# First chunk of a layer norm ahead of attention and MLP: the order of normalisation, statistics and piece copies on VectorE and ScalarE, and epsilon as the root's bias

## The chip, the cores and the metric

The kernel runs on one core of a Trainium2 chip. The metric is the device time of one execution in microseconds (us); several runs are made and the median is taken. The core has five engines with queues of their own: TensorE (PE, with its weight loads as PEld), VectorE (DVE), ScalarE (ACT), GpSimd (POOL) and SyncE (SP), which here issues the DMAs. They meet through semaphores only.

## The reference, cut to what matters

```
x: 2048 x 640
xn  = (x - mean(x)) / sqrt(var(x) + 1e-5)            # over the 640 columns
A   = sliding-window attention(xn @ wqkv) @ wo       # 32 heads of 20, window 256
B   = (gelu(xn @ w_gate) * (xn @ w_up)) @ w_down     # 640 -> 1728 -> 640
out = x + A + B
```

All of it is float32. The kernel splits a float32 operand into a high piece (a rounded copy, made by ScalarE) and a low piece (the remainder, by a subtraction on VectorE or GpSimd) and multiplies high by high, low by high and high by low.

## The kernel before

The 2048 rows are 16 tiles of 128 rows, and four tiles are a chunk. First every chunk is normalised, transposed and projected; attention, gate and up projections and the down projection follow. The change lies in the first of these stages, above all in its first chunk.

For a tile `xi` of 128 x 640, `ln_stats` (L119 to L121) makes mean and variance on VectorE: two statistics instructions and one that joins them into `mv`. `ln_sqrt` adds epsilon on VectorE (L126, `ve`) and takes the root on ScalarE (L127, `sq`). `ln_rstd` makes the reciprocal and one Newton step with four small VectorE instructions (L132 to L135): the reciprocal reads `sq`; the other three each read both `ve` and `rs` from SBUF. `ln_apply` (L139) subtracts the mean and multiplies, in place, over 640 columns.

```
        nc.vector.tensor_scalar(ve, mv[:, :, 1], EPS, None, op0=OP.add)
        nc.scalar.activation(sq, ve, AF.Sqrt)
```

`turn` (L156) then transposes 128-column blocks of the normalised tiles on TensorE into PSUM (`ps_t`), where the high piece `xh` is copied out by ScalarE (`high`, L292, in the first chunk, L164 in the others) and the low piece `xl` is subtracted by VectorE (`low`, L289 and L165). Weights are split by `split`: the high piece `wqh` on ScalarE (L74), the low piece `wql` on GpSimd (L75). `load_v` does the same with the value weights: `wvh` on ScalarE (L238), `wvl` on GpSimd (L239), five pieces of 320 columns each. GpSimd also fills constants: `mask`, `nm`, the ones columns of `v` (L249, L250), and `ones` (L365).

`first_chunk` is the only code that works on half a chunk at a time: tiles 0 and 1 (`ta`, the first pair) and tiles 2 and 3 (`tb`, the second pair). It projects two weight tiles, `w0` and `w5`, into the PSUM tiles `dn` (L296). Its TensorE order is: ten transposes of the first pair, five matmuls `w0` high by `xh`, five `w5` high by `xh`, five `w0` low by `xh`, six transposes of the second pair, five `w5` low by `xh`, four transposes, then forty more matmuls. Then come the value projections of the first tiles (`ps_v`, L82). The results go through `save_qk`, which splits them in pieces too (L215 on ScalarE, L216 on VectorE, L203 on ScalarE, L204 on GpSimd) and stores them. 64 small matmuls on a zero tile (L355, `ps_u`) run ahead of everything while the first tiles are loaded.

What sets the order: inside `first_chunk` the order on TensorE, ScalarE and VectorE is the order of the code, except where an independent instruction of another part (the `identb` copy L361, the `wvh` copies) is set between. GpSimd and SyncE there, and all engines in the chunks 1 to 3 behind it, are ordered by a scheduler from its own estimates. Each engine then works through its queue strictly in that order. From about 50 us on, the order of all engines is the same in both kernels.

Of the kernel before, what the change touches and what calls it, by code (L numbers as in the profile page):

```python
# [9 lines left out]
F32 = mybir.dt.float32  # L10
F32R = mybir.dt.float32r
BF = mybir.dt.bfloat16
AF = mybir.ActivationFunctionType
OP = mybir.AluOpType
# [7 lines left out]
KT = D // 128  # L22
# [3 lines left out]
EPS = 1e-5  # L26
# [19 lines left out]
def block_kernel(ctx, tc, x, xt, wqk, wv, wo, wgu, wd, wdl, out):  # L46
    nc = tc.nc

    const = ctx.enter_context(tc.tile_pool(name="const", bufs=1))
# [4 lines left out]
    nc.scalar.activation(one, one, AF.Sqrt)  # L54
    ident = const.tile([128, 128], F32, name="ident")
    make_identity(nc, ident)
    edge = ctx.enter_context(tc.tile_pool(name="edge", bufs=1, side="right"))
    edge.tile([128, 120], F32, name="edge")
    px = ExitStack()
# [11 lines left out]
    def split(pool, raw, shape, name, lo_eng, bufs=None):  # L71
        hi = pool.tile(shape, F32R, name=name + "h", tag=name + "h", bufs=bufs)
        lo = pool.tile(shape, F32R, name=name + "l", tag=name + "l", bufs=bufs)
        nc.scalar.activation(hi, raw, AF.Copy)  # L74
        lo_eng.tensor_tensor(out=lo, in0=raw, in1=hi.bitcast(F32), op=OP.subtract)  # L75
        return hi, lo
# [20 lines left out]
    vp = pr.enter_context(tc.tile_pool(name="vp", bufs=5, side="right"))  # L97
    st1 = pr.enter_context(tc.tile_pool(name="st1", bufs=1, side="right"))
    identb = st1.tile([128, 256], BF, name="identb")[:, 0:128]
    mask = st1.tile([128, 384], F32, name="mask")  # L100
    nc.gpsimd.memset(mask, 0.0)
    nc.gpsimd.affine_select(out=mask, in_=mask, pattern=[[1, 384]], compare_op=OP.is_ge,
# [9 lines left out]
    def ln_load(t, lp):  # L112
        xi = lp.tile([128, D], F32, name="xi", tag="xi", bufs=8)
        nc.sync.dma_start(xi, x[t * 128:(t + 1) * 128, :])
        return xi

    def ln_stats(xi, mv, lp):
        st = lp.tile([128, 2, 6], F32, name="st", tag="st", bufs=4)
        nc.vector.bn_stats(st[:, 0, :], xi[:, 0:320])  # L119
        nc.vector.bn_stats(st[:, 1, :], xi[:, 320:640])  # L120
        nc.vector.bn_aggr(mv, st)  # L121

    def ln_sqrt(mv, n, lp):
        ve = lp.tile([128, n], F32, name="ve", tag="ve", bufs=2)
        sq = lp.tile([128, n], F32, name="sq", tag="sq", bufs=2)
        nc.vector.tensor_scalar(ve, mv[:, :, 1], EPS, None, op0=OP.add)  # L126
        nc.scalar.activation(sq, ve, AF.Sqrt)  # L127
        return ve, sq

    def ln_rstd(ve, sq, n, lp):  # L130
        rs = lp.tile([128, n], F32, name="rs", tag="rs", bufs=4)
        nc.vector.reciprocal(rs, sq)  # L132
        nc.vector.tensor_tensor(out=ve, in0=ve, in1=rs, op=OP.mult)
        nc.vector.scalar_tensor_tensor(ve, ve, -0.5, rs, op0=OP.mult, op1=OP.mult)
        nc.vector.scalar_tensor_tensor(rs, ve, 1.5, rs, op0=OP.add, op1=OP.mult)  # L135
        return rs

    def ln_apply(xi, mv, rs):
        nc.vector.tensor_scalar(xi, xi, mv[:, 0:1], rs, op0=OP.subtract, op1=OP.mult)  # L139
# [11 lines left out]
    def turn(k, xs, where):  # L151
        n = len(xs)
        pool, tag = {"x": (psx, "ex"), "m": (psm, "mx"), "o": (pso, "o")}[where]
        ps = pool.tile([128, n * 128], F32, name="ps_t", tag=tag)
        for i in range(n):
            nc.tensor.transpose(ps[:, i * 128:(i + 1) * 128], xs[i][:, k * 128:(k + 1) * 128], ident)  # L156
        return ps
# [22 lines left out]
    def load_qk(t):  # L180
        raw = wrp.tile([128, KT, 128], F32, name="wr", tag="wr")
        nc.sync.dma_start(raw, wqk[t])
        return raw

    def split_qk(raw):
        return split(wp, raw, [128, KT, 128], "wq", nc.gpsimd)
# [98 lines left out]
    def first_chunk(xs, wr0, wr5, lp):  # L285
        halves = slice(0, 256), slice(256, 512)

        def low(k, ps, cs):
            nc.vector.tensor_tensor(out=xl[:, k, cs], in0=ps, in1=xh[:, k, cs].bitcast(F32), op=OP.subtract)  # L289

        def high(k, ps, cs):
            nc.scalar.activation(xh[:, k, cs], ps, AF.Copy)  # L292

        def part(ps, w, r, cs, first=False, last=False):
            for k in range(KT):
                nc.tensor.matmul(ps[:, cs], w[:, k, :], r[:, k, cs], start=first and k == 0,  # L296
                                 stop=last and k == KT - 1, skip_group_check=True)

        with tc.manual_schedule(engines=MANUAL):
            mv = [lp.tile([128, 2, 2], F32, name="mv", tag="mv", bufs=2) for _ in range(2)]  # L300
            ln_stats(xs[0], mv[0][:, 0, :], lp)
            ln_stats(xs[1], mv[0][:, 1, :], lp)
            va = ln_sqrt(mv[0], 2, lp)
            ln_stats(xs[2], mv[1][:, 0, :], lp)
            rs = ln_rstd(*va, 2, lp)
            ln_apply(xs[0], mv[0][:, 0, :], rs[:, 0:1])
            ln_apply(xs[1], mv[0][:, 1, :], rs[:, 1:2])
            ln_stats(xs[3], mv[1][:, 1, :], lp)
            w0 = split_qk(wr0)
            w5 = split_qk(wr5)  # L310
            ta = [turn(k, xs[0:2], "xmxmm"[k]) for k in range(KT)]
            dn = [psd.tile([128, C], F32, name="ps_d", tag="dn") for _ in range(2)]
            for k in range(KT):
                high(k, ta[k], halves[0])
                if k == 1:
                    vb = ln_sqrt(mv[1], 2, lp)
            for k in range(2):
                low(k, ta[k], halves[0])
            rs = ln_rstd(*vb, 2, lp)
            ln_apply(xs[2], mv[1][:, 0, :], rs[:, 0:1])  # L320
            ln_apply(xs[3], mv[1][:, 1, :], rs[:, 1:2])
            part(dn[0], w0[0], xh, halves[0], True)
            part(dn[1], w5[0], xh, halves[0], True)
            part(dn[0], w0[1], xh, halves[0])
            tb = [turn(0, xs[2:4], "o")]
            for k in range(2, KT):
                low(k, ta[k], halves[0])
            for k in range(1, 3):
                tb.append(turn(k, xs[2:4], "oxmxm"[k]))
            part(dn[1], w5[1], xh, halves[0])  # L330
            for k in range(3, KT):
                tb.append(turn(k, xs[2:4], "oxmxm"[k]))
            for k in range(KT):
                high(k, tb[k], halves[1])
            for k in range(KT):
                low(k, tb[k], halves[1])
            mv = lp.tile([128, 4, 2], F32, name="mv4", tag="mv4", bufs=2)
            for i, w in enumerate((w0, w5)):
                part(dn[i], w[0], xl, halves[0])
                part(dn[i], w[0], xh, halves[1])  # L340
                part(dn[i], w[1], xh, halves[1])
                part(dn[i], w[0], xl, halves[1], last=True)
                for j in range(2):
                    ln_stats(xs[4 + 2 * i + j], mv[:, 2 * i + j, :], lp)
                save_qk(5 * i, 0, dn[i])
        return w0, w5, mv

    v0 = []
    with tc.tile_pool(name="lp", bufs=1, side="right") as lp:
        xs = [ln_load(t, lp) for t in range(4)]  # L350
        warm = lp.tile([128, 256], BF, name="warm")[:, 0:128]
        nc.vector.memset(warm, 0.0)
        ps = psd.tile([128, C], F32, name="ps_u", tag="dn")
        for i in range(WARM):
            nc.tensor.matmul(ps[:, 0:128], warm, warm, start=True, stop=True)  # L355
        wr0, wr5 = load_qk(0), load_qk(5)
        prep = load_v(0, v0, lp)
        next(prep)
        xs += [ln_load(t, lp) for t in range(4, 8)]
        w0, w5, mv1 = first_chunk(xs, wr0, wr5, lp)  # L360
        nc.vector.tensor_copy(identb, ident)  # L361
        run(prep)
        v0 = v0[0]
        ones = lp.tile([2, 2 * C], BF, name="ones")
        nc.gpsimd.memset(ones, 1.0)  # L365
        for i in range(NK):
            for j in (0, 2):
                nc.sync.dma_start(ks[i][120:122, j:j + 2].rearrange("p j t -> p (j t)"), ones)
        for c in range(1, NC):
            ln_scale(xs[4 * c:4 * c + 4], lp, mv1 if c == 1 else None)  # L370
            ln_turn(4 * c, xs[4 * c:4 * c + 4])
            if c + 1 < NC:
                xs += [ln_load(t, lp) for t in range(4 * c + 4, 4 * c + 8)]
            if c == 2:
                raws1 = [load_qk(1), load_qk(6)]
            if c < NC - 1:
                run(*[proj_v(v0, 4 * c - 4 + i, None if i % 2 else (pso, "o")) for i in range(4)])
                run(proj_qk(0, w0, c), proj_qk(5, w5, c))
# [761 lines left out]
```

## Time and profile before

| | |
|---|---|
| median of 3 runs | 1117.17 us (1116.29 to 1118.18) |
| the profiled execution | 1116.69 us, its span 1115.0 us |
| TensorE busy | 1098.7 us, 99% of the span |
| VectorE, ScalarE, GpSimd busy | 637.7, 470.9 and 359.9 us |
| mean granted TensorE clock | 0.995 |

The page's chain is the work that ended last, followed back from the last instruction. A row of the timeline has the start, the length, the engine, the line and operation, what is written and read with its shape, a count where several were merged, and in brackets the idle time of the engine before it and what ended that. The start of an instruction is the moment at which the engine takes it up; one that cannot go on is shown as a long one. A row of the windows has, for each stretch of time, the length and the busy times of the five engines with their instruction counts, then the granted TensorE clock as a share of full speed, the DMA share and the GB/s.

### The profile page before, as it was taken

The page shows a single profiled execution, that of the slowest core. Times are in us where ns is not written, and L with a number is a line of the kernel's source. Part 1 is how long each engine was busy: PE and PEld are TensorE (multiplying, and loading weights), DVE is VectorE, ACT ScalarE, POOL GpSimd, SP SyncE. Part 2 cuts the span into 40 slices and gives each one's busy share as a digit, 9 for nine tenths or more (in the row PEclk, how much of TensorE's full clock was granted, in tenths as well). Part 3 has the DMA queues.
Part 4 walks back from the last instruction along what each step waited for, and adds up shares of the span by engine and source line. Part 5 has one row for each costly group of instructions (what it writes and reads, how often), then busy time and mean ns, then how long its engine had stood idle before and what let it go on. Part 6 is the DMA issues. An engine that isn't in the chain of part 4 may idle for free.

```text
span 1115.0 us, 19319 instructions
## 1 busy us (share of the span) xinstructions
PE 1098.7 (99%) x6802; PEld 837.6 (75%) x6802; DVE 637.7 (57%) x1736; ACT 470.9 (42%) x952; POOL 359.9 (32%) x504
## 2 busy tenths in 40 slices
PE   7999999999999999999999999999999999999998
PEld 7887666767668876667667676788888878788886
DVE  7856676757648577586777775566664350211203
ACT  4434554555555455645545454643323421211111
POOL 4122542644552233534323343311113313222230
PEclk8999999999999999999999999999999999999999
DMA  4642343543443314343242431342214835152431
GB/s 157 220 143 60 103 144 115 139 146 95 139 144 109 87 58 143 111 146 107 80 140 83 125 104 38 107 150 92 89 66 157 264 125 175 48 179 75 152 95 66
DMA packets 76145, 133.10 MB, mean 119 GB/s; under 512 B 12800, under 2 KB 33664, under 8 KB 76048
## 3 DMA queue, kind: packets, MB, share of 16 engines
q1 hardware_dynamic: 76048, 131.87, 37.6%
q8 instruction: 53, 0.87, 0.3%
q14 instruction: 44, 0.36, 0.1%
HBM read 86.31 MB, written 44.83 MB: 118 GB/s over the span
## 4 chain that ended last, share of the span: by engine, by line
PE 91%; DVE 4%; ACT 1%; DMA 1%; issue 1%; POOL 1%; SPq 0%; DVEq 0%; ACTq 0%; POOLq 0%
PE ps_d L82 28%; PE ps_w L942 23%; PE ps_g L851 11%; PE ps_o L484 7%; PE ps_e L462 7%; PE ps_m L410 6%; PE ps_v L82 6%; DVE junk L412 2%; PE ps_g L82 1%; PE ps_t L156 1%; PE ps_d L296 1%; ACT P L464 1%; PE ps_b L912 0%; DMA xi<-x 0%; DMA qs<-qd 0%
## 5 line engine op out<-in xcount | busy, mean ns | idle before, releaser
L412 DVE CUSTOM_DVE_ANT_0 junk<-ps_m,mask 128x384 bf16<-128x384 f32 (+2 forms) x512 | 271.2, 530 | 158.0 <-PE ps_m L410 120.0
L464 ACT ACTIVATE P<-ps_e 128x512 f32<-128x512 f32 (+2 forms) x384 | 197.5, 568 | 71.0 <-PE ps_e L462 64.6
L470 POOL TENSOR_SCALAR_AFFINE_SELECT P<-P 128x512 f32<-128x512 f32 x128 | 83.8, 655 | 221.1 <-ACT P L464 212.8
L82 PE MATMUL ps_d<-xh,wqh 128*128 128x512 f32 x510 | 150.4, 407 | 0.0
L82 PE MATMUL ps_d<-xh,wql 128*128 128x512 f32 x510 | 150.3, 407 | 0.0
L82 PE MATMUL ps_d<-xl,wqh 128*128 128x512 f32 x510 | 149.3, 406 | 0.0
L410 PE MATMUL ps_m<-ks,qs 120*128 120x128 bf16 (+1 forms) x704 | 120.9, 275 | 4.1 <-DVE mx L412 2.8
L921 POOL TENSOR_TENSOR ht<-hr,ht 128x512 fp32r<-128x512 f32 x52 | 69.2, 1337 | 172.1 <-ACT ht L919 142.9
L462 PE MATMUL ps_e<-qs,ks 122*128 122x128 bf16 (+2 forms) x704 | 112.5, 277 | 0.8 <-ACT P L464 0.6
L82 PEld LDWEIGHTS ps_d<-xl,wqh 128*128 128x128 f32 x510 | 92.9, 188 | 19.2 <-issue 2.4
L82 PEld LDWEIGHTS ps_d<-xh,wql 128*128 128x128 f32 x510 | 93.1, 189 | 18.0 <-issue 0.9
L82 PEld LDWEIGHTS ps_d<-xh,wqh 128*128 128x128 f32 x510 | 92.6, 188 | 17.2 <-ACT xh L164 0.3
L919 ACT ACTIVATE ht<-hr 128x512 fp32r<-128x512 f32 x56 | 35.1, 629 | 132.7 <-PE ps_w L942 80.8
L462 PEld LDWEIGHTS <-ks 122*128 122x128 bf16 x704 | 49.9, 98 | 54.6 <-issue 44.3
L473 POOL TENSOR_SCALAR_AFFINE_SELECT P<-P 128x512 f32<-128x512 f32 x112 | 74.2, 673 | 51.2 <-ACT P L464 51.2
L410 PEld LDWEIGHTS <-qs 120*128 120x128 bf16 x704 | 62.1, 98 | 33.1 <-issue 13.7
L484 PE MATMUL ps_o<-P,v 128*32 128x384 f32 (+2 forms) x1408 | 84.3, 386 | 0.0
L204 POOL TENSOR_TENSOR pt<-r,pt 128x512 bf16<-128x512 f32 x40 | 47.3, 1181 | 105.1 <-ACT pt L203 104.8
L484 PEld LDWEIGHTS ps_o<-P,v 128*32 128x32 f32 x1408 | 40.1, 110 | 39.6 <-issue 32.8
L923 DVE TENSOR_TENSOR ht<-hr,ht 64x512 fp32r<-64x512 f32 x4 | 2.8, 690 | 112.3 <-ACT ht L919 112.3
L515 POOL TENSOR_TENSOR wql<-wr,wqh 128x128 fp32r<-128x128 f32 x115 | 51.6, 481 | 38.0 <-ACT wqh L510 38.0
L488 ACT ACTIVATE ob<-ps_o 128x512 f32<-128x512 f32 x32 | 19.1, 597 | 101.1 <-PE ps_o L484 58.5
(270 smaller groups left out, 1889.2 us busy)
## 6 DMA issues: line engine op xcount, KB each, us to landing
hd<-he SPq DMA_DIRECT2D x52, 256.0 KB
hr<-hd SPq DMA_DIRECT2D x52, 256.0 KB
wr<-wgu SPq DMA_DIRECT2D x27, 320.0 KB
qs<-qd SPq DMA_DIRECT2D x32, 240.0 KB
ks<-kd SPq DMA_DIRECT2D x32, 240.0 KB
xi<-x SPq DMA_DIRECT2D x16, 320.0 KB
qs<-qd SPq DMA_DIRECT2D x32, 160.0 KB
ks<-kd SPq DMA_DIRECT2D x32, 160.0 KB
```

The costliest lines, as they stand in the source:

```text
L82: nc.tensor.matmul(ps, a(k), b(k), start=n == 0, stop=n == 3 * nk - 1)
L410: nc.tensor.matmul(ps[:, lo:hi], lh, rhs, start=True, stop=True)
L412: nc.vector.tensor_tensor_reduce(out=junk[:, 0:n], in0=ps[:, 0:n], in1=mask[:, 384 - n:384], scale=1.0, scalar=NEG, op0=OP.add, op1=OP.max ...
L462: nc.tensor.matmul(ps[:, col:col + n], k[0:QROWS, j, kc:kc + 128], q[0:QROWS, j, q0:q0 + n], start=True, stop=True)
L464: nc.scalar.activation(pt[:, j, lo:hi], ps[:, lo:hi], AF.Exp, scale=SCALE)
L470: nc.gpsimd.affine_select(out=a, in_=a, pattern=[[0, 4], [1, 128]], compare_op=OP.is_ge, fill=0.0, base=0, channel_multiplier=-1)
L473: nc.gpsimd.affine_select(out=a, in_=a, pattern=[[0, 4], [-1, 128]], compare_op=OP.is_ge, fill=0.0, base=-1, channel_multiplier=1)
L484: nc.tensor.matmul(o[32 * j:32 * j + 32, q0:q0 + n], v[:, w0_:w0_ + 32], pt[:, j, col:col + n], start=i == 0, stop=i == len(todo) - 1, ski ...
L515: nc.gpsimd.tensor_tensor(out=lo[:, k], in0=raw[:, k], in1=hi[:, k].bitcast(F32), op=OP.subtract)
L851: nc.tensor.matmul(ps, i, j, start=first and n == 0, stop=n == len(work) - 1, skip_group_check=True)
L921: nc.gpsimd.tensor_tensor(out=t[:, 1, :], in0=raw, in1=t[:, 0, :].bitcast(F32), op=OP.subtract)
L942: nc.tensor.matmul(pss[m], w[:, ms], r, start=first and j == 0, stop=last and j == len(work) - 1)
```

## The change

In the first chunk the second pair's statistics of tile 2 leave their place between the first root and its reciprocal, so that the first pair is normalised straight away; both tiles' statistics follow. On ScalarE the first two `xh` copies go ahead of the two weight splits, one each, and the second root goes behind all five copies. The root takes the variance itself and epsilon as its bias, and the sum `ve`, which only the Newton step reads now, is made beside it, as an addition of two tensors. `identb` is copied on GpSimd at the start and no longer on VectorE behind the first chunk. `ln_sqrt` serves the other chunks as well.

```diff
+    eps = const.tile([128, 4], F32, name="eps")
+    nc.vector.memset(eps, EPS)
...
+    nc.gpsimd.tensor_copy(identb, ident)
...
     def ln_sqrt(mv, n, lp):
         ve = lp.tile([128, n], F32, name="ve", tag="ve", bufs=2)
         sq = lp.tile([128, n], F32, name="sq", tag="sq", bufs=2)
-        nc.vector.tensor_scalar(ve, mv[:, :, 1], EPS, None, op0=OP.add)
-        nc.scalar.activation(sq, ve, AF.Sqrt)
+        nc.scalar.activation(sq, mv[:, :, 1], AF.Sqrt, bias=eps[:, 0:1])
+        nc.vector.tensor_tensor(out=ve, in0=mv[:, :, 1], in1=eps[:, 0:n], op=OP.add)
         return ve, sq
...
             ln_stats(xs[0], mv[0][:, 0, :], lp)
             ln_stats(xs[1], mv[0][:, 1, :], lp)
-            va = ln_sqrt(mv[0], 2, lp)
-            ln_stats(xs[2], mv[1][:, 0, :], lp)
-            rs = ln_rstd(*va, 2, lp)
+            rs = ln_rstd(*ln_sqrt(mv[0], 2, lp), 2, lp)
             ln_apply(xs[0], mv[0][:, 0, :], rs[:, 0:1])
             ln_apply(xs[1], mv[0][:, 1, :], rs[:, 1:2])
+            ln_stats(xs[2], mv[1][:, 0, :], lp)
             ln_stats(xs[3], mv[1][:, 1, :], lp)
-            w0 = split_qk(wr0)
-            w5 = split_qk(wr5)
             ta = [turn(k, xs[0:2], "xmxmm"[k]) for k in range(KT)]
             dn = [psd.tile([128, C], F32, name="ps_d", tag="dn") for _ in range(2)]
-            for k in range(KT):
+            high(0, ta[0], halves[0])
+            w0 = split_qk(wr0)
+            high(1, ta[1], halves[0])
+            w5 = split_qk(wr5)
+            for k in range(2, KT):
                 high(k, ta[k], halves[0])
-                if k == 1:
-                    vb = ln_sqrt(mv[1], 2, lp)
+            vb = ln_sqrt(mv[1], 2, lp)
             for k in range(2):
                 low(k, ta[k], halves[0])
             rs = ln_rstd(*vb, 2, lp)
...
-        nc.vector.tensor_copy(identb, ident)
```

In the built program other things move with it. GpSimd's fills of `nm`, of four `v` tiles and of `ones` come ahead of `wql` instead of behind it. On ScalarE all five `wvh` copies stand right behind the second root, ahead of the second pair's `xh` copies (before: four ahead of them and one between them). On SyncE the loads of tiles 8 and 9 come earlier, among the stores of the first chunk's results. In chunk 1 statistics of tile 8 stand between the small instructions of `ln_rstd` on VectorE; in chunk 2 two of the four L139 come ahead of an L216 and two behind it, where before one L216 stood ahead of all four.

## The prediction

> **What bounds the kernel now.** Read in this order: the page's chain, TensorE's waits, the timeline of the first 40 us, windows of 1 us, and one line elsewhere that shows the same collision.
>
> ```profile
> PE 91%; DVE 4%; ACT 1%; DMA 1%; issue 1%; POOL 1%; SPq 0%; DVEq 0%; ACTq 0%; POOLq 0%
> ```
>
> The chain that sets the end is TensorE's nearly throughout, so what the change can win is TensorE idle or slow time in the first chunks. TensorE's waits:
>
> ```profile
> PE ps_d L296 <- ACT xh L292: 2.8, 1, 2.8
> ...
> PE ps_t L156 <- DVE xi L139: 2.6, 3, 1.5
> ```
>
> The timeline (start, length, what) tells where these two come from:
>
> ```profile
> 9.25 3.04 POOL L75 TENSOR_TENSOR wql<-wr,wqh 128x640 fp32r<-128x640 f32 x2 [6.34 <-DMA wr<-wqk]
> ...
> 9.95 0.93 DVE L361 CAST identb<-ident 128x128 bf16<-128x128 f32 x1
> ...
> 11.03 2.77 DVE L126 TENSOR_SCALAR ve<-mv 128x2 f32<-128x2 f32 x1
> ...
> 12.76 1.01 POOL L365 MEMSET ones<- 2x1024 bf16 x1
> ...
> 13.83 0.20 ACT L127 ACTIVATE sq<-ve 128x2 f32<-128x2 f32 x1 [3.35 <-DVE xl L289]
> ...
> 14.36 2.20 PE L296 MATMUL ps_d<-xh,wqh 128*128 128x256 f32 x8 [2.79 <-ACT xh L292]
> ...
> 14.86 1.86 DVE L139 TENSOR_SCALAR xi<-xi,mv,rs 128x640 f32<-128x640 f32 x2
> 15.29 0.91 POOL L239 TENSOR_TENSOR wvl<-wvall,wvh 128x320 fp32r<-128x320 f32 x1 [1.45 <-ACT wvh L238]
> ...
> 16.25 2.85 POOL L239 TENSOR_TENSOR wvl<-wvall,wvh 128x320 fp32r<-128x320 f32 x3
> ...
> 17.43 1.48 PE L156 MATMUL ps_t<-ident,xi 128*128 128x128 f32 x6
> ```
>
> The addition of epsilon (L126) is a 128x2 operation; at 5.83 it took 0.17 us, here 2.77. It stands still until 13.80, when GpSimd's wql and the memsets behind it are through. The second root waits for it, three xh copies stand behind the root on ScalarE, and TensorE waits 2.79 us for them. One of the two L139 is stretched likewise (1.86 for two; the first pair took 1.14) while wvl runs. The same collision far away, 32 times (least, median, greatest ns):
>
> ```profile
> L418 DVE SCALAR_TENSOR_TENSOR nm<-mx,nm x32: 175/548/550, 82.9 to 687.7; 128x16 bf16<-128x16 f32 x32
> ```
>
> There GpSimd's selects run back to back (some 635 ns each). L417 ends with one, the next select has started some 0.1 us before L418 is issued, and L418 waits for nearly all of it. So a VectorE instruction with two SBUF inputs waits for a reading GpSimd instruction, and a chain of them pays one GpSimd instruction per link. The last view is the clock (seventh number after the busy times of the five engines):
>
> ```profile
> 9.00:10.00 1.00, 0.87 (x6) 0.71 (x6) 1.00 (x4) 0.96 (x3) 0.75 (x1) 0.84 0.97 406
> ...
> 12.00:13.00 1.00, 0.00 (x0) 0.00 (x0) 1.00 (x3) 0.00 (x0) 1.00 (x10) 0.50 1.05 417
> ...
> 19.00:20.00 1.00, 1.00 (x7) 1.00 (x7) 0.78 (x2) 0.69 (x2) 0.34 (x2) 0.54 0.02 4
> ```
>
> From 9.68 to 19.92 TensorE runs at half clock: a 256-column matmul comes every 0.213 us (16.36 to 17.43 for five) against 0.12 later (20.88 to 21.48 for five).
>
> **The change, part by part.** *First root.* Without L126 ahead of it, it starts at 5.83 instead of 6.04. Without the third tile's statistics between root and reciprocal, the reciprocal starts at 6.07 instead of 7.37, and with the same 0.73 us behind it L139 starts at 6.80 (8.10) and the second tile is ready at 7.94 (9.24). The transposes of the first pair move from 9.29 to 8.00. Gain here: 1.3 us on this chain, none at the end yet.
>
> *ScalarE.* The first xh copy comes at 8.37 (8.00 plus 0.33 for the transpose plus the 0.04 to ScalarE). Its 0.26 us go ahead of the first weight split, whose load had landed at 8.43 in any case; wqh runs 8.63 to 9.37 (before 8.43 to 9.16). The second copy, the second wqh (load landed at 9.18), three copies and the root follow: copies done at 11.1, root 11.0 to 11.2. Nothing on this path waits for VectorE's epsilon, and the 2.79 us wait goes.
>
> *TensorE up to there.* First matmuls from 9.43, the fifth at 11.2, then five of w5 and five with wql (GpSimd 9.45 to 11.0): done by 12.5 at full clock, 13.3 at half. Before, the same fifteen end at about 17.5.
>
> *What is late next: the transposes of the second pair (17.43 before).* In the built order GpSimd does its memsets before the weights, so wql takes 9.45 to 11.0 and 10.95 to 12.5, two memsets of 0.12 and 0.25 follow, and the five wvl (0.87 each) come at once, because wvh now stands right behind the root (wvall landed at 11.14 by its completion counts, wvh done from 11.6). GpSimd is full of reading instructions to about 17. VectorE's new epsilon addition is a TENSOR_TENSOR with two SBUF inputs: issued at 10.0, it ends with the first wql at 11.0. Two xl subtractions (PSUM and one SBUF input; L289 was not stretched at 16.64 beside wvl) end at 11.7. The reciprocal ends at 11.8, the multiply waits for the second wql: 12.5. Then two scalar_tensor_tensor and two L139 meet wvl. If the first slips in during the memsets, it ends at 12.7, the next with the first wvl at 13.55, the first L139 after the second wvl at 14.8, the last after the third at 16.07. If it does not, all is one wvl later: 16.9. Transposes at 16.1 or 17.0. I take the middle, and both ends for the range: there is no row of before with a two-input VectorE instruction beside a memset alone.
>
> A page has a rule for that race, the Trainium skill's "SBUF — State Buffer", section "Who interferes with whom": two SBUF inputs collide with a GpSimd instruction that reads SBUF, not with one that only writes. By that rule the first one passes the memsets and the transposes come at 16.1. The same section speaks against the change, since it trades the one-input tensor_scalar for an instruction with two SBUF inputs; the trace agrees in L418.
>
> *TensorE from there to the first ps_v (25.08).* Before: 7.65 us, 2.49 of them at half clock, so 6.41 at full. After, with the clock back at 19.92 as before: from 16.1, 3.82 at half do 1.91, the other 4.50 end at 24.42 (−0.66); from 17.0 it is 24.87 (−0.21). Middle −0.4.
>
> *Chunk one.* In before a 0.65 us wait at 29.85, behind L133 held by GpSimd's L204 (27.57 to 28.74). The scheduler now puts statistics of tile 8 between the scalar_tensor_tensor. The last of these meets L204 and ends with it, as L133 did; 0.4 of statistics come after instead of 0.4 of arithmetic. No change (−0.1 to +0.4; tile 8 is loaded some 10 us ahead, so its landing adds nothing).
>
> *Chunk two.* TensorE waited 0.39 and 0.09 us at 44.55 and 45.07, because L139 stood behind an L216 and was held by L204. In the new order two L139 come before L216 and the other two right behind it, at some 43.3, ahead of the end of the projections at 44.2: −0.45 (0 at worst).
>
> *Nothing for the rest:* the eps memset (some 0.1 us, at 1.1 under the loads), identb on GpSimd (some 0.4 us at 2.5, where it then idles to 9.2), the earlier ones and tile loads (the DMA share is 0.03 or less from 14 to 20), and the other later epsilon steps (0.15 to 0.16 us either way). Behind 50 us every engine's order is the same, and TensorE's other waits are local, so a shift is kept to the end.
>
> Sum: −0.4 − 0.45, about −0.85 us on the profiled run's 1116.69 (span 1115.0 and 1.69 around it): 1115.8. The median of before is 0.48 above that run, so the forecast is 1116.3. A measurement can tell some 0.2%, 2.2 us, from no change; this is less.
>
> **Rivals.** *The collision is milder.* If VectorE wins the lock at each link, or wvall lands some 2 us later, the chain ends at 14.1 and the transposes start at 14.15. With the clock back at 19.92: 2.88 done at half by then, 3.53 more, 23.45, −1.6; if the idle time, only 1.6 us, does not cost the clock at all: 20.6, −4.5. With chunk two −2.1 to −5.0: 1112.2 to 1115.1. For it: the CAST got in between the two wql. Against: L418, 30 of 32 times.
>
> *Slower: the clock stays down longer.* TensorE now idles 3.6 to 4.5 us in one piece (2.79 before). In before the clock returned 5.56 us after work resumed. If transposes start at 17.0 and it takes as long, the clock is back at 22.56: 2.78 done by then, 3.63 more, 26.2, +1.1; and if ordinary runs of before get it back some 2 us sooner than the profiled one, the comparison loses another 1.1: +1.1 to +2.2, with chunk two not gained 1118.3 to 1119.4. It decides from a start near 16.5 on with the clock's return later than about 22. For it: that profiled stall left the clock at 0.50. Against: at 19.92 it returned though TensorE had worked only since 14.36.
>
> By the Trainium skill's "TensorE: Matmul & The Clock Gate", Part 1, the gate judges free-running windows of 3413 ns, so the return depends on where the windows fall in an execution. The trace agrees that 10.24 us at half is three such windows; a stall longer than one window would by that rule always cost the clock, which the forecast has.
>
> *No shift at all:* the transposes are pinned at 17 and chunk two keeps its wait. 1117.2.
>
> **Numbers.** Forecast (16.1 to 17.0, within 1115 to 1117.5) 0.58, milder 0.22, longer half clock 0.13, no shift 0.07. Beyond 2.2 us faster lies nearly all of the milder case and a little of the forecast: 0.24. Beyond 2.2 slower, half of the clock case and unknown effects of shifted loads: 0.09. The range leaves out the far ends of both: 1113.0 to 1118.8.
>
> **Right or wrong by the profile after:** first L139 at 6.8; no ScalarE root behind a VectorE epsilon; no 2.79 wait at L296 but one of 3 to 4.5 us at the second pair's transposes; the multiply, one or both scalar_tensor_tensor and both L139 stretched to the end of a wql or wvl; ps_v first at 24.4 to 24.9; no wait near 44. Wrong, if the second L139 ends before 15, or the half clock lasts past 22.

## The result, and the profile after

The changed kernel is slower: 1127.5 us in the median of four runs (1126.92 to 1128.83) against 1117.51 us for the kernel before (four runs, 1116.29 to 1118.18). The ratio is 1.0095, with a 95% interval of 1.0082 to 1.0108. The forecast was 1116.3 us, and the range ended at 1118.8. The profiled execution took 1127.97 us, its span is 1126.3 us.

In the changed kernel the lines move: L126 and L127 become L130 and L129, L132 to L135 become L135 to L138, L139 is L142, L75 is L77, L239 is L242, L156 is L159, L296 is L299, L82 is L84, and L851 and L942 are L853 and L944.

Part 1 of the page of after (TensorE busy was 1098.7 us before), and its chain of work by engine:

```profile
PE 1111.0 (99%) x6802; PEld 836.5 (74%) x6802; DVE 639.0 (57%) x1736; ACT 471.4 (42%) x952; POOL 361.4 (32%) x505
...
PE 90%; DVE 6%; issue 1%; ACT 1%; DMA 1%; POOL 1%; SPq 0%; DVEq 0%; POOLq 0%; ACTq 0%
```

TensorE does the same 6802 matmuls and is busy 12.3 us longer; the span is 11.3 us longer. So the loss is no wait: the matmuls themselves take longer. TensorE's waits of after (what waited, for what, total us, times, longest) have nothing of that size:

```profile
PE ps_t L159 <- DVE xi L142: 4.0, 4, 2.0
...
PE ps_d L299 <- ACT xh L295: 0.5, 1, 0.5
```

The timeline of after, first chunk:

```profile
7.28 1.14 DVE L142 TENSOR_SCALAR xi<-xi,mv,rs 128x640 f32<-128x640 f32 x2
...
9.93 3.07 POOL L77 TENSOR_TENSOR wql<-wr,wqh 128x640 fp32r<-128x640 f32 x2 [5.28 <-ACT wqh L76]
...
10.48 1.01 DVE L130 TENSOR_TENSOR ve<-mv,eps 128x2 f32<-128x2 f32 x1
...
12.26 0.77 DVE L136 TENSOR_TENSOR ve<-ve,rs 128x2 f32<-128x2 f32 x1
...
12.99 0.23 POOL L253 MEMSET v<- 128x64 f32 x1
13.06 0.16 DVE L137 SCALAR_TENSOR_TENSOR ve<-ve,rs 128x2 f32<-128x2 f32 x1
13.10 4.64 POOL L242 TENSOR_TENSOR wvl<-wvall,wvh 128x320 fp32r<-128x320 f32 x5
13.26 0.72 DVE L138 SCALAR_TENSOR_TENSOR rs<-ve,rs 128x2 f32<-128x2 f32 x1
14.01 2.18 DVE L142 TENSOR_SCALAR xi<-xi,mv,rs 128x640 f32<-128x640 f32 x2
15.18 0.33 PE L159 MATMUL ps_t<-ident,xi 128*128 128x128 f32 x1 [1.99 <-DVE xi L142]
```

This is the chain that was forecast, link by link: L130 ends with the first `wql`, L136 with the second, L137 slips in, and L138 and the two L142 run beside `wvl`. The first of the fifteen 256-column matmuls starts at 9.90 (forecast 9.43), the last ends at 13.2 (forecast 12.5 at full clock, 13.3 at half); of the 2.79 us wait for the third `xh` copy 0.5 us is left. Three of the 1-us windows, the same stretches as before:

```profile
9.00:10.00 1.00, 0.78 (x8) 0.54 (x5) 0.96 (x4) 1.00 (x3) 0.07 (x1) 1.00 0.96 389
...
12.00:13.00 1.00, 1.00 (x11) 0.98 (x9) 0.97 (x3) 1.00 (x4) 1.00 (x3) 1.00 0.91 355
...
19.00:20.00 1.00, 1.00 (x7) 1.00 (x6) 0.73 (x2) 0.62 (x2) 0.00 (x0) 0.52 0.00 0
```

TensorE is busy from 12 to 13, at the full clock, where it stood still before; half clock lasts from 16.55 to 19.97 only (9.67 to 19.91 before).

Now the loss. The answers for single tiles give a line's count, the least, median and greatest duration in ns, and the first and last start in us. Before:

```profile
L82 PE MATMUL ps_v<-wvh,xh x160: 302/309/446, 25.1 to 397.4; 128*128 128x320 f32 x160
...
L851 PE MATMUL ps_g<-xh,wqh x90: 389/389/389, 729.1 to 850.8; 128*128 128x512 f32 x90
...
L942 PE MATMUL ps_w<-ht,wd1h x40: 389/389/389, 854.9 to 1052.6; 128*128 128x512 f32 x40
...
L942 PE MATMUL ps_w<-ht,wd3h x40: 389/389/389, 862.1 to 1059.4; 128*128 128x512 f32 x40
...
L942 PE MATMUL ps_w<-ot,wo3h x40: 387/389/397, 909.8 to 1110.2; 128*128 128x512 f32 x40
```

After:

```profile
L84 PE MATMUL ps_v<-wvh,xh x160: 304/309/447, 24.2 to 397.4; 128*128 128x320 f32 x160
...
L853 PE MATMUL ps_g<-xh,wqh x90: 395/395/396, 732.2 to 857.5; 128*128 128x512 f32 x90
...
L944 PE MATMUL ps_w<-ht,wd1h x40: 389/389/396, 861.6 to 1062.8; 128*128 128x512 f32 x40
...
L944 PE MATMUL ps_w<-ht,wd3h x40: 393/396/397, 868.8 to 1069.8; 128*128 128x512 f32 x40
...
L944 PE MATMUL ps_w<-ot,wo3h x40: 387/389/397, 917.6 to 1121.4; 128*128 128x512 f32 x40
```

Read the starts first. At the first `ps_v` after is 0.9 us ahead; at the last (397.4) the lead is gone; at the first `ps_g` of this line it is 3.1 us behind, at the last 6.7, and at the end 11.2. So the loss is no single event: between the first and the last of these `ps_g` alone, 122 us, 3.6 us are lost. Then the durations: `ps_g` went from 389 to 395 ns, and so did `ps_w` with `wd3`, but not with `wd1`, not `ps_w` from `ot`, and not the 320-column `ps_v`. (The durations overlap; from one start to the next it is 226 to 227 ns before and 233 to 234 after.)

What differs in the memory: the new tile `eps` has 16 bytes per partition, for which the first pool of SBUF's left side sets 32 aside. In the built program every left-hand tile behind it lies 32 bytes higher: the weights `wqh` at 7200 instead of 7168, `ht` at 35360 instead of 35328, the stationary tiles `s1` to `s4` of `ps_g`, and `wd0` and `wd1`. The right-hand tiles `xh`, `xl`, `wd2` to `wd13`, `wo` and `ot` have not moved. A matmul here has two operands in SBUF: the stationary one (128x128; a row LDWEIGHTS loads it ahead of the matmul) and the moving one (128x512). Of the 512-column matmuls, the slower ones are those with one operand on each side. The 320-column `ps_v` (moving `wvh`, stationary `xh`) has one on each side too and is not slower.

### The profile page after: what moved, and what is told of

Same layout as the page of the kernel before. It is cut to its first block, busy times and chain, and to the rows that moved or that the text cites. A ratio compares the mean times of both kernels' runs of the same rounds, so it can differ in the third digit from the quotient of the medians.

```text
span 1126.3 us, 19319 instructions
## 1 busy us (share of the span) xinstructions
PE 1111.0 (99%) x6802; PEld 836.5 (74%) x6802; DVE 639.0 (57%) x1736; ACT 471.4 (42%) x952; POOL 361.4 (32%) x505
## 4 chain that ended last, share of the span: by engine, by line
PE 90%; DVE 6%; issue 1%; ACT 1%; DMA 1%; POOL 1%; SPq 0%; DVEq 0%; POOLq 0%; ACTq 0%
PE ps_d L84 27%; PE ps_w L944 23%; PE ps_g L853 11%; PE ps_o L486 7%; PE ps_e L464 7%; PE ps_m L412 6%; PE ps_v L84 6%; DVE junk L414 2%; PE ps_g L84 1%; PE ps_t L159 1%; DMA wr<-wqk 1%; ACT P L466 0%; PE ps_b L914 0%; DVE xi L142 0%; PE ps_d L299 0%
## 5 line engine op out<-in xcount | busy, mean ns | idle before, releaser
L84 PE MATMUL ps_d<-xh,wqh 128*128 128x512 f32 x510 | 152.0, 410 | 0.0
L84 PE MATMUL ps_d<-xh,wql 128*128 128x512 f32 x510 | 151.9, 410 | 0.0
L84 PE MATMUL ps_d<-xl,wqh 128*128 128x512 f32 x510 | 151.0, 409 | 0.0
L84 PEld LDWEIGHTS ps_d<-xl,wqh 128*128 128x128 f32 x510 | 92.9, 189 | 19.7 <-issue 2.1
L84 PEld LDWEIGHTS ps_d<-xh,wql 128*128 128x128 f32 x510 | 93.2, 189 | 18.5 <-issue 0.6
L84 PEld LDWEIGHTS ps_d<-xh,wqh 128*128 128x128 f32 x510 | 92.6, 188 | 18.1 <-ACT xh L167 0.3
```

The costliest lines, as they stand in the source:

```text
L84: nc.tensor.matmul(ps, a(k), b(k), start=n == 0, stop=n == 3 * nk - 1)
```

## Experiments

Ratios are against runs of the kernel before on the same chip; its medians there were 1116.8 to 1117.3 us, so medians of different chips can be set side by side to some 0.5 us.

**Is it the address, and what is the reordering worth alone?** `aligned` is the changed kernel with no new tile:

```diff
-    one = const.tile([128, 96], F32, name="one")
-    eps = const.tile([128, 4], F32, name="eps")
+    both = const.tile([128, 96], F32, name="one")
+    one, eps = both[:, 0:92], both[:, 92:96]
```

> The changed kernel with epsilon kept in the last four columns of the tile `one`, so that no tile is added and every tile lies at the address it had before; instructions and their order as in the changed kernel. Address theory (the 10 us come from the new tile, which moves all tiles on the left of SBUF by 32 bytes and with them the operands of the 512-column matmuls): those matmuls come every 226 to 230 ns again and the time is 1.2 us under before, about 1116.3, ratio 0.998 to 0.9995. Order theory (the changed order, the loads moved in the queues, or epsilon's new arithmetic cost it somewhere behind the first chunk): the time stays at 1126 to 1128, ratio 1.008 to 1.010.

Measured: 1115.81 us (11 runs), ratio 0.9991 (0.9982 to 1.0000). Its page has TensorE busy 12.6 us less than after, and its span, 1113.7, is 12.6 us shorter:

```profile
PE 1098.4 (99%) x6802; PEld 836.4 (75%) x6802; DVE 639.6 (57%) x1736; ACT 471.1 (42%) x952; POOL 360.6 (32%) x505
```

The counterpart, `before_pad32`, is the kernel before with nothing but an unused tile of 32 bytes:

```diff
     make_identity(nc, ident)
+    const.tile([128, 8], F32, name="pad")
```

> The kernel before with one tile of 32 bytes a partition added behind `ident`, which nothing writes or reads. Instructions and order stay those of before. Address theory: the drift comes without any of the change: 512-column matmuls at 232 to 235 ns, 1128 to 1130, ratio 1.009 to 1.012. Order theory: nothing happens, 1117.5, ratio 1.000.

Measured: 1129.62 us (4 runs), ratio 1.0110 (1.0096 to 1.0124). Three of its groups (busy time in us, mean ns of one, idle time before):

```profile
L852 PE MATMUL ps_g<-xh,wqh 128*128 128x512 f32 x90 | 30.7, 395 | 0.0
...
L943 PE MATMUL ps_w<-ot,wo3h 128*128 128x512 f32 x40 | 13.6, 389 | 0.0
...
L943 PE MATMUL ps_w<-ht,wd3h 128*128 128x512 f32 x40 | 13.2, 395 | 0.0
```

From start to start, `ps_g` and the `ps_w` with an operand on each side take 233 to 235 ns, `ps_d` 235 (230 in before), the `ps_w` of `ot` 227. An unused tile costs 12 us; the change without its tile costs nothing. The address is the cause.

**By how much must it be off?** First the changed kernel with a bigger `eps` tile, 64 and 128 bytes:

```diff
-    eps = const.tile([128, 4], F32, name="eps")
+    eps = const.tile([128, 16], F32, name="eps")[:, 0:4]      # after_eps64
+    eps = const.tile([128, 32], F32, name="eps")[:, 0:4]      # after_eps128
```

> The changed kernel with 64 bytes for epsilon's tile instead of 16. Left-hand tiles lie 64 bytes further than before. Address theory with 64-byte pieces: time as with the old addresses, about 1116.3, matmuls at 227 to 230 ns. Address theory with larger pieces (128 bytes or more): still 1126 to 1129. Order theory: 1126 to 1128.

> The same with 128 bytes. Address theory with pieces of 64 or 128 bytes: about 1116.3. With larger ones: 1126 to 1129. Order theory: 1126 to 1128.

Measured: 1126.31 us, ratio 1.0084 (1.0070 to 1.0097), and 1126.9 us, ratio 1.0088 (1.0074 to 1.0102). Neither cures it. At 64 bytes the spacing is 233 in `ps_g`, but in `ps_w` 227 to 229 with the high pieces of `wd2` to `wd11` and 232 with most of their low pieces; at 128 bytes it is 231 to 233 in all of these. Then downwards, by a shorter `one` in `aligned`:

```diff
-    both = const.tile([128, 96], F32, name="one")
-    one, eps = both[:, 0:92], both[:, 92:96]
+    both = const.tile([128, 32], F32, name="one")      # minus256
+    one, eps = both[:, 0:28], both[:, 28:32]
+    both = const.tile([128, 48], F32, name="one")      # minus192
+    one, eps = both[:, 0:44], both[:, 44:48]
```

> The aligned version with the tile `one` cut from 384 to 128 bytes per partition, so that every left-hand tile lies 256 bytes lower than before (nothing else changes; the warm-up square root and memset of `one` cover fewer columns). If the pace of a matmul depends on its operands' addresses in units of 256 bytes or a divisor of it that 128 is not, the 512-column matmuls keep their 227 ns and the time stays at 1115.8 +- 1.5 us. If the unit is 512 bytes or more, the groups ps_g<-xh,wqh, ps_g<-xh,s and ps_w<-ht,wd show 231 to 235 ns and the time is 1123 to 1128 us. If only the distance from the address in the kernel before matters (any shift costs), the same slow time.

> As the version with the tile `one` cut, with 192 bytes of it left: every left-hand tile lies 192 bytes lower than in the kernel before. If the pace repeats every 256 bytes, this is the same as 64 bytes higher, and its pattern must come back: ps_d<-xh,wq 235 ns in the median, ps_g<-xh,s and ps_g<-xh,wq 233 to 234, but ps_w<-ht,wd 226; time 1124.5 to 1127 (aligned plus 10.5). If not (a period of 512 or none), the pattern is another; if the shift by 256 was harmless only because it went downwards, all of them show 227 and the time is 1115.8.

Measured: `minus256` 1115.62 us, ratio 0.9988 (0.9979 to 0.9997), every group at 226 to 227 as before. `minus192` 1125.08 us, ratio 1.0067 (1.0052 to 1.0083), and the peculiar pattern of 64 bytes is back, the split between high and low pieces too. So the pace repeats every 256 bytes, whether the tiles are moved up or down.

**Each operand, or the distance between the two?** `moving32` is `aligned` with `ht`, the moving operand of `ps_w`, shifted by 32 bytes together with `wd0` and `wd1`, and the rest of that stage by 512:

```diff
+    p2.enter_context(tc.tile_pool(name="padc", bufs=1)).tile([128, 8], F32, name="padc")
     cp = p2.enter_context(tc.tile_pool(name="cp", bufs=1, reuse_waits="tile"))
...
+    p2.enter_context(tc.tile_pool(name="padd", bufs=1)).tile([128, 120], F32, name="padd")
     c2s = ExitStack()
```

> The aligned version with 32 unused bytes ahead of the feed-forward stage's left-hand pool and 480 unused bytes behind it: ht (the moving operand of ps_w<-ht,wd), sel and the weights wd0 and wd1 lie 32 bytes higher, everything that follows (the selected stationary tiles s1 to s4, q, u1) 512 bytes higher, the attention stage and the q and k weights as before. Theory that the address of each operand counts, moving as well as stationary, and that 512 bytes are harmless: ps_w<-ht,wd goes from 227 to 233 to 235 ns, ps_g<-xh,s and ps_d stay at 226 to 230, and the time is that of aligned plus about 210 to 230 matmuls' three passes: some 4 to 5 us, 1119.5 to 1121. Rival, that only the stationary operand counts: ps_w<-ht,wd slower only for wd0 and wd1, under 1 us in all. Rival, that any shift counts: ps_g<-xh,s at 233 too, about 2 us more.

Measured: 1121.24 us, ratio 1.0042 (1.0028 to 1.0055), 5.4 us above `aligned`. `ps_g` keeps its 389 ns, and of `ps_w` this:

```profile
L946 PE MATMUL ps_w<-ht,wd1h x40: 389/389/396, 854.1 to 1055.5; 128*128 128x512 f32 x40
...
L946 PE MATMUL ps_w<-ht,wd3h x40: 393/396/397, 861.6 to 1062.5; 128*128 128x512 f32 x40
```

A shifted moving operand is enough, against the rival. But none of the three theories had `wd1` right: it was shifted together with `ht` and is not slow, as in after. That points to the distance between the operands. Two more runs tell that apart, by the unused tile on the right-hand side, which the kernel before has already: `both32` is the changed kernel, `right32` the kernel before, each with

```diff
-    edge.tile([128, 120], F32, name="edge")
+    edge.tile([128, 112], F32, name="edge")
```

> The changed kernel with its unused right-hand tile `edge` 32 bytes smaller, so that the right-hand tiles (xh, xl, wd2 to wd13, wo, ot) lie 32 bytes higher too, as the left-hand ones do: every 512-column matmul has both operands 32 bytes off their place in the kernel before. Theory that the distance between the two operands' addresses, modulo 256, sets the pace (in the changed kernel wd0 and wd1, shifted like ht, keep 227 ns, wd2 to wd13, not shifted, take 233 to 234): all groups return to 227 (ps_d 230), PE busy is about 1098.5 us, and the time is 1114.8 to 1116.8, that of the aligned version. Rival, that each operand must start at a multiple of 256 by itself: everything stays at 233 to 235, ps_w<-ot,wo goes from 227 to 233 too and ps_v may slow down, 1127.5 to 1131.

> The kernel before with only that smaller `edge`: right-hand tiles 32 bytes higher, left-hand tiles in their place. Distance theory: the pairs of a left-hand and a right-hand tile (ps_d<-xh,wq, ps_g<-xh,s, ps_w<-ht,wd2 to wd13) take 231 to 235 ns, the pair of two right-hand tiles (ps_w<-ot,wo) and the pair of two left-hand ones (ps_w<-ht,wd0 and wd1) 227; time 1124 to 1130. Rival, that each operand counts by itself: ps_w<-ot,wo at 233 or more, wd0 and wd1 at 227.

Measured: `both32` 1115.64 us, ratio 0.9988 (0.9978 to 0.9997); `right32` 1129.02 us, ratio 1.0108 (1.0091 to 1.0125). The tile lines of `both32`, where all operands are 32 bytes off their old place:

```profile
L853 PE MATMUL ps_g<-xh,wqh x90: 389/389/389, 728.2 to 849.9; 128*128 128x512 f32 x90
...
L944 PE MATMUL ps_w<-ht,wd3h x40: 389/389/389, 861.1 to 1058.4; 128*128 128x512 f32 x40
```

and of `right32`, where only the right-hand ones are:

```profile
L851 PE MATMUL ps_g<-xh,wqh x90: 393/396/398, 732.6 to 857.9; 128*128 128x512 f32 x90
...
L942 PE MATMUL ps_w<-ht,wd1h x40: 389/389/397, 862.0 to 1063.1; 128*128 128x512 f32 x40
...
L942 PE MATMUL ps_w<-ht,wd3h x40: 394/396/397, 869.1 to 1070.1; 128*128 128x512 f32 x40
...
L942 PE MATMUL ps_w<-ot,wo3h x40: 388/389/394, 917.9 to 1121.7; 128*128 128x512 f32 x40
```

The distance decides. In `right32` the pair of two right-hand tiles (`ot`, `wo3`) was shifted as a whole and keeps 389, the pair of two left-hand ones (`ht`, `wd1`) keeps it too, and every mixed pair is slow. The changed kernel is repaired by moving what it did not move.

One thing stays open. In after, three matmuls of the pair `ot`, `wo4` are followed by one of the pair `ht`, `wd0`. Each pair lies on one side of SBUF, and yet the steps from there on take 235, 230, 224, 231, 236, 228, 232 and 231 ns before they settle at 226 to 227 (the three times agree within 1 ns); in before and in `both32` they take 225 to 228. So the operands of neighbouring matmuls count too. The next stationary operand is loaded while a matmul runs: a row LDWEIGHTS starts some 2 ns after the start of the matmul ahead of it. Whether the distance that matters is that to a matmul's own stationary operand or to the next one's, these runs do not tell.

**What each half of the change does.** Both with all addresses as before. `reorder` is `aligned` with epsilon added on VectorE ahead of the root, as in the kernel before; `epsonly` is the kernel before with the new `ln_sqrt` only:

```diff
# reorder, against aligned
-        nc.scalar.activation(sq, mv[:, :, 1], AF.Sqrt, bias=eps[:, 0:1])
-        nc.vector.tensor_tensor(out=ve, in0=mv[:, :, 1], in1=eps[:, 0:n], op=OP.add)
+        nc.vector.tensor_scalar(ve, mv[:, :, 1], EPS, None, op0=OP.add)
+        nc.scalar.activation(sq, ve, AF.Sqrt)
# epsonly, against before: the opposite
```

> The aligned version without its epsilon part: epsilon is added on VectorE by a one-input tensor_scalar and the root waits for it, as in the kernel before; only the order is the new one (first pair normalised before the next statistics, copies ahead of the second root, identb on GpSimd). Theory (tensor_scalar stands still for reading and for write-only GpSimd work alike, a two-input tensor_tensor only for reading work): the second addition, issued at about 10.1, ends at about 12.9 with the memsets instead of 11.2, the second root at 13.2 instead of 11.4; wvh stands behind it on ScalarE, so wvl starts about 2 us later too, and the second pair's transposes start within 1 us of aligned's 14.8 and 15.9: 1115.3 to 1117. Rival, that the order alone removes the wait: the addition takes about 0.2 us and the transposes start at 12 to 13, 1113 to 1114.5.

> The kernel before with only the epsilon part of the change (root straight from the variance with epsilon as bias, epsilon added by tensor_tensor; epsilon in the last four columns of the tile `one`, so all addresses as before). Theory: the second root no longer waits for VectorE (about 11.1 instead of 13.8 us), so the 2.8 us wait of the first projection for its third xh copy goes; but the two-input addition ends with the second wql (12.3), and wvh right behind the root lets wvl start near 12.8, beside the second normalisation; transposes of the second pair at 15 to 16.5 instead of 17.4: 0.3 to 1.2 us faster than before, 1115.9 to 1116.9. Rival, that the order is needed for any gain: 1117.0 +- 0.5.

Measured: `reorder` 1115.88 us, ratio 0.9984 (0.9976 to 0.9993), as fast as `aligned` within the intervals. Its addition:

```profile
10.17 3.08 POOL L76 TENSOR_TENSOR wql<-wr,wqh 128x640 fp32r<-128x640 f32 x2 [5.52 <-ACT wqh L75]
...
10.72 1.01 DVE L128 TENSOR_SCALAR ve<-mv 128x2 f32<-128x2 f32 x1
```

It ended at 11.73, with the first `wql`, and not with the memsets, so that detail of the expectation was wrong (the long memsets come earlier in this order). `epsonly` 1118.81 us, ratio 1.0017 (1.0008 to 1.0025): slower than before, where a gain was expected. Its timeline:

```profile
13.26 0.68 DVE L135 TENSOR_TENSOR ve<-ve,rs 128x2 f32<-128x2 f32 x1
13.97 0.89 DVE L136 SCALAR_TENSOR_TENSOR ve<-ve,rs 128x2 f32<-128x2 f32 x1
...
14.89 1.68 DVE L137 SCALAR_TENSOR_TENSOR rs<-ve,rs 128x2 f32<-128x2 f32 x1
...
16.61 1.63 DVE L141 TENSOR_SCALAR xi<-xi,mv,rs 128x640 f32<-128x640 f32 x2
```

The root is early, at 11.2, so the wait for the third copy falls from 2.8 to 0.7 us; but `wvl` starts earlier too, the second normalisation meets it at every link, and the transposes start at 17.77 (17.43 before) after a wait of 3.8 us. The loss shows better against `before_pad32`, which has the order of before and, like `epsonly`, 3.4 us of half clock (before itself has 10.2): there the transposes start at 16.82 and `ps_v` at 24.18, here at 17.77 and 26.26. All of the gain is the order's; epsilon as a bias adds nothing to it that these runs can tell.

**A version that beats both.** The second normalisation still runs beside `wvl`. `early` is `aligned` with the value weights' split issued behind the second pair's copies; `early2` also moves the second q/k weight's split behind the second root; `early3` is `early` with two of the five `wvh` copies behind the third of the second pair's copies:

```diff
             for k in range(KT):
                 high(k, tb[k], halves[1])
+            run(prep)
...
-        w0, w5, mv1 = first_chunk(xs, wr0, wr5, lp)
-        run(prep)
+        w0, w5, mv1 = first_chunk(xs, wr0, wr5, lp, prep)
```

> The aligned version with the first value weights' ScalarE copies (five, L241) issued behind the second pair's five high-part copies instead of ahead of them, so that GpSimd's five subtractions wvl start at about 18.5 instead of 12.8 us and no longer run beside the second pair's normalisation on VectorE. Theory (those subtractions hold the two-input and the tensor_scalar instructions on VectorE): the step L138 takes 0.16 instead of 0.71 us, the two L142 0.61 instead of 1.11 and 1.15, so the second pair's transposes start about 1.6 us earlier (13.2 and 13.8 instead of 14.8 and 15.9), and the time is 0.8 to 1.8 us below aligned, 1114.0 to 1115.0. Rival: wvl, now done at about 24, is late for the first value projection (its fifth to tenth matmul, from 24.2 us on), which gives the gain back: 1115.5 to 1117.

> As early, and the second q/k weight's split (ScalarE copy, GpSimd subtraction) is issued behind the second square root, so that its GpSimd pass starts at about 12 instead of 11.1 us. Theory: the step L136 (0.77 us beside that pass) falls to 0.16, but the pass now runs beside the two L142; a gain of at most 0.3 us over early, 1113.8 to 1115.0, or a loss of up to 0.6 us if the tensor_scalar instructions are held to the end of the pass (transposes then at about 14.0 us, and the matmuls of the second weight wait for its copy).

> As early, with two of the five ScalarE copies wvh issued behind the third of the second pair's high-part copies instead of behind the fifth. In early the first wvl starts at 17.2 us, and the five of them (4.25 us) followed by GpSimd's L207 lead to chunk one's normalisation. Theory: wvl starts at about 16.3 and ends at 20.6, L207 at 20.7 to 21.8, which brings chunk one's transposes forward by 0.6 to 0.8 us: 1112.8 to 1113.4. Rival: the two remaining high-part copies, 0.4 us later, hold TensorE, and nothing is gained: 1113.6 to 1114.

Measured: `early` 1113.63 us (10 runs), ratio 0.9972 (0.9963 to 0.9981); `early2` 1114.09, 0.9975 (0.9966 to 0.9984); `early3` 1113.8, 0.9967 (0.9955 to 0.9980). The timeline of `early`:

```profile
12.91 0.16 DVE L137 SCALAR_TENSOR_TENSOR ve<-ve,rs 128x2 f32<-128x2 f32 x1
13.11 0.16 DVE L138 SCALAR_TENSOR_TENSOR rs<-ve,rs 128x2 f32<-128x2 f32 x1
13.31 1.13 DVE L142 TENSOR_SCALAR xi<-xi,mv,rs 128x640 f32<-128x640 f32 x2
```

Without `wvl` beside them L138 takes 0.16 and the two L142 1.13 us instead of 0.72 and 2.18, as the theory of the collision has it. `ps_v` starts at 20.93 (23.87 in `aligned`), and the clock stays at full. The transposes start at 13.98 and 14.50, 0.9 and 1.4 us earlier than in `aligned` and not 1.6, and yet the median lies below the expected range, 2.2 us under that of `aligned`.

More than half of that is the clock, which the expectation left out. In all ten executions of `early` the granted clock was 1.000. Of the 32 executions of `aligned`, `minus256` and `reorder`, which differ in the first chunk at most by the root, it was 0.999 or more in 11; these took 1114.4 us in the median, the other 21 took 1116.1. The 1.7 us between them are half of one stretch of 3.4 us at half clock. So against an execution that keeps its clock `early` gains some 0.8 us. It keeps the clock with waits of 0.92 and 0.19 us at the second pair's transposes, where `aligned` has 1.98 and 0.74. A part of the lead is lost again in chunk one: `wvl`, now from 17.2 to 21.5, stands ahead of the subtraction whose results its normalisation waits for, and its transposes wait 1.15 us (0.53 in `aligned`). In `early2` the expectation failed at L136: issued at 12.38, it met the delayed second `wql` and took 1.13 us. `early3` brings chunk one's transposes from 26.20 to 25.56, but it did not reach the expected 1112.8 to 1113.4, and the end of the three versions cannot be told apart.

## Why the prediction was wrong

The step that failed is "Nothing for the rest: the eps memset (some 0.1 us ...)", with the sentence behind it, "Behind 50 us every engine's order is the same, ... so a shift is kept to the end". The new tile was costed by the instruction that fills it. Its price is its 32 bytes: 12.6 us of matmul time (after less `aligned`), in the projections, the gate and up and the down projections behind the first chunk, whose matmuls the change leaves as they are. By the rows, the mixed pairs come to about that: 1530 `ps_d` with 3 ns more in the mean, 600 `ps_g` and 700 `ps_w` with some 6.5 ns more each, 4.6 + 3.9 + 4.6, some 13 us. The sentence on the order is not quite right either (SyncE's DMA issues still change places up to 101 us), but `aligned` has the same SyncE order without the loss. The rivals were all waits and clocks of the first 50 us, and none was priced above 1119.4.

Point by point, the rest held in kind. First L139 at 6.8: 7.28; the statistics ahead of it ended 0.33 us later in this execution (6.13, 5.80 before), and the root with a bias took 0.30 instead of 0.20 us. No root behind epsilon: right. No 2.79 us wait at L296, but one at the second pair's transposes: right in kind, 1.99 and 0.74 us instead of 3 to 4.5 in one, since each tile's transposes start when that tile is ready. The collision: L137 passed the memsets, L138 ended with the first `wvl`, the first L142 at 15.1 and the last at 16.19, forecast 14.8 and 16.07. By the Trainium skill's "SBUF — State Buffer", section "Who interferes with whom", an instruction with two SBUF inputs does not wait for a GpSimd instruction that only writes: L137 agrees (0.16 us beside L253). In `epsonly` it does not hold: L135, also with two SBUF inputs, took 0.68 us and ended with the 2x1024 bf16 memset of `ones` (12.95 to 13.97), one case. The prediction's other reading of that section, that giving up the one-input tensor_scalar speaks against the change, did not come true: with one SBUF input L126 had stood for 2.77 us, and the addition took 1.01 us in either form.

First `ps_v` at 24.4 to 24.9: 24.20 here, 23.87 in `aligned`. That is partly luck: the forecast took over the end of the half clock, 19.92, from the run of before, and here it ended at 19.97. In `minus256` and `reorder`, whose first chunk is the same but for the root, there was no half clock and `ps_v` started at 22.5 and 22.9, and their medians are the same as `aligned`'s within the interval. No wait near 44: 0.09 us of 0.48 is left. The sum of these steps, −0.85 us for 1116.3, fits what `aligned` and `both32` measure: 1115.81 and 1115.64, 1.2 us below their runs of before; the intervals reach from 2.5 us below to none. The shift is kept to the end once the operands are in their places. Longer half clock, as a rival, did not come: it lasted at most 3.4 us in every profiled run of the new order, and from 3.4 to 10.2 us in those with the order of before.

## What to carry to other kernels

Ahead of costing a change by its instructions, compare where the tiles lie: a new tile of a few bytes in an early pool moves all that follow it on its side, and here that cost ten times what the change was worth. Where a profile shows the same matmuls slower by a constant few ns, with no wait, look at the addresses of the two operands, and at what the padding tiles of the kernel were holding in place; keep small constants in the slack of a tile that exists. And an instruction held by another engine is better helped by moving that engine's work away (`early`, 2.2 us) than by taking one link off the chain (epsilon as a bias: nothing). Compare executions by their granted clock before crediting such a gain to the chain: here 1.7 us went with one stretch of half clock.

## What the runs showed of the hardware

- The pace of a 512-column matmul on float32 pieces (fp32r in the rows) depends on the distance between its stationary and its moving operand in SBUF, modulo 256 bytes. In `ps_g` and `ps_w`, from start to start: 226 to 227 ns with nothing moved and with one operand moved by −256 or 512; 233 to 234 in the mean with one of them moved by 32, whichever it is (single groups 231 to 235); 231 to 233 at 128. At 64 and −192 it is 233 in `ps_g`, where the stationary operand is the one moved, and 226 to 233 in `ps_w`, by the tile. Where each lies by itself is no matter (both shifted by 32: 227). Behind a change of pair it took six to eight matmuls to settle. 320-column matmuls (147 to 148 ns) and weight loads (187 to 190 ns) do not show it.
- The Trainium skill's "TensorE: Matmul & The Clock Gate", section "Step-by-step: what each phase is for", says that the streaming operand and the weight load have a read port each and that loading weights takes no read bandwidth from the running matmul. The runs show an interaction between the two operands, 3% of the pace; whether it lies in the reads, and why 64 bytes part high from low pieces, stays open.
- A VectorE instruction with one SBUF input is held by a reading GpSimd instruction no less than one with two: the addition of epsilon took 1.01 us both as a tensor_scalar (`reorder`) and as a tensor_tensor (after), ending with `wql`. In before the one-input form stood until 13.80, 1.5 us past the end of the last `wql` (12.29), beside memsets that only write; in `epsonly` the two-input form ended with the last `wql`, at 12.49, though memsets ran on. One case each.
- A wait of 2.0 us and a further 0.7 us at the second pair's transposes was followed by 3.4 us at half clock in six profiled executions (after, `aligned`, `both32`, `moving32`, `after_eps64`, `minus192`) and by none in three (`minus256`, `reorder`, `after_eps128`).
